# Weight blocks converted step by step inside the attention, its results in a ring outside the pool

## The chip, the core and the metric

The kernel runs on one core of a Trainium2 chip. The core has five engines that each take their instructions in program order and meet only through semaphores: TensorE (PE in the profile, its weight loads PEld), VectorE (DVE), ScalarE (ACT), GpSimd (POOL) and SyncE (SP), which here issues nearly all DMAs. The metric is the time of one execution on the device in microseconds. A run varies by some tenths of a per cent; about 1% is taken as what separates a change from none.

## What is computed

Three stages follow one another: attention with capped scores, a gated MLP, and a mixture of experts.

```python
def _attn_ref(q, k, v, cap):                  # 4 batches, 12 heads, 448 tokens, 64 wide
    scores = cap * np.tanh(scale * q @ k.T / cap)
    attn = np.exp(scores - max); attn /= attn.sum(-1) + 1e-9
    return attn @ v

def _moe_ref(x, w_in, w_out):                 # 1792 tokens, 768 -> 2048 -> 768
    h = x @ w_in
    return (h * (1.0 / (1.0 + np.exp(-h)))) @ w_out

def _moe2_ref(x, w_skip, w_gate, w1, w2):     # 8 experts, one for each token
    ...
```

The MLP's weights arrive as 64-bit floats. The kernel reads them as pairs of 32-bit words and makes 32-bit floats of them on the chip.

## The kernel before

**Attention.** Two heads form a `Unit` (24 units: 4 batches of 6). Two units form a quad of 7 chunks; a `Chunk4` is 128 keys of both heads of a unit, or the 64 keys that are left over from both units. `slot4(p)` handles two chunks, and there are `SL` = 42 slots with scores. In a slot ScalarE does `weigh` (tanh, then exp, of 128 x 896 values, for each of two chunks); TensorE does `av` of the slot before, the denominators (`den`) of units whose sums are made, and the scores of the next slot; VectorE does a first sum (`sum1`), reciprocals of denominators and the products `xf` (`finish`), and, for the first two batches, a cast `x_h`; GpSimd does the second sum (`sum2`), the sums of the leftover keys (`sum_rest`) and, for the first two batches, the subtraction `x_l`. So a unit's denominator on TensorE needs sums from VectorE and GpSimd of the slot before. For batches 2 and 3 `xf` is stored to `xd` in DRAM by SyncE. The instructions are issued in the order in which the code is written; nothing reorders them. The engines keep that order.

**Precision.** A matmul of the MLP is made of three, with a high and a low part of weights and data: `wh` times `x_h`, `wh` times `x_l`, `wl` times `x_h`.

**Conversion of a weight block.** `fetch` loads the 64-bit block `raw` (768 KB, 2 buffers). `ready` makes `wr` (3 buffers): magnitude on ScalarE (line 392), clamp on VectorE (393), scaling of the low word on ScalarE (394), shift and mask on VectorE (396), sign on VectorE (397), and an add on GpSimd (398). `split` stores `wr` for later use (`keep`), casts it to `wh` on ScalarE (407) and subtracts on GpSimd to `wl` (410). `tick_a(k)` splits block k+1, `tick_b(k)` makes block k+3 ready and fetches block k+5. Each call issues the whole conversion at once. In the attention this happens for blocks 0 to 2 at slots 31, 34 and 38, with fetches at 28 and 29.

**From the attention to the MLP.** After the last slot with scores come the first MLP matmuls, `h_start(0,0,0)` (18 matmuls of block 0 with batch 0), then `slot4(SL)`, the last chunks' products and sums, `h_start(0,0,1)` and `slot4(SL + 1)`, the last denominator. `h_end` makes of such a result `ph` the pair `gh`, `gl`: tanh on ScalarE, a product on VectorE, a cast on ScalarE, a subtraction on VectorE. Then the attention's pool `ap`, where `xf` lies in two buffers, is closed, and pools for `gh` and `gl` are opened in the space that came free. `h_end(0,1)` is the first to write there. A ring is a piece of a tile in the pool `mp`, which lives on, taken in turn by `turn_of`; the ring `xt` has four places of 448 columns, and before the change only the MLP's second half uses it.

The rest of the program, MLP and experts, is not touched.

Of the kernel before, what the change touches and what calls it, by code (L numbers as in the profile page):

```python
# [1 line left out]

# [6 lines left out]
F32 = mybir.dt.float32  # L9
F32R = mybir.dt.float32r  # L10
I32 = mybir.dt.int32
U32 = mybir.dt.uint32
AF = mybir.ActivationFunctionType
ALU = mybir.AluOpType
AX = mybir.AxisListType

P = 128
B, H, S, D = 4, 12, 448, 64
# [20 lines left out]
WC = DM  # L39
# [20 lines left out]
def kernel(  # L60
# [13 lines left out]
    nc = tc.nc  # L74
# [17 lines left out]
    def turn_of(t):  # L92
        ring = scr[t]
        ring[3] = (ring[3] + 1) % ring[2]
        return ring[0][:, ring[3] * ring[1] : (ring[3] + 1) * ring[1]]
# [28 lines left out]
    class Unit:  # L124
# [72 lines left out]
            nc.vector.reciprocal(self.rd, pden[:, :S])  # L197

        def finish(self):
            xf = ap.tile([P, S], F32, tag="xf", name=f"xf{self.n}")  # L200
            nc.vector.tensor_tensor(xf, self.pav[:, :S], self.rd, op=ALU.mult)
            self.xf = xf
            if self.b >= 2:
                nc.sync.dma_start(xd[self.b - 2, self.hp], xf)
# [139 lines left out]
    def slot4(p):  # L344
        for c in chunks4[2 * p : 2 * p + 2]:
            c.weigh()
        late = chunks4[2 * p - 2 : 2 * p] if p else []
        for c in late:
            c.av()
        due = open_[:]  # L350
        open_.clear()
        for c in late:
            if (u := c.sums()) is not None:
                open_.append(u)
        closing()
        for u in due:
            u.den()
            done.append(u)
        for c in chunks4[2 * p + 2 : 2 * p + 4]:
            c.score()  # L360
        for c in chunks4[2 * p : 2 * p + 2]:
            quad = c.i // (2 * KF + 1)
            for u in units[2 * quad + 2 : 2 * quad + 4]:
                if c.c == 0:
                    u.load()
                elif c.c == KF:
                    u.load_v()

    class Chunk:
# [30 lines left out]
        def split(self):  # L400
            if self.wh is not None:
                return
            w = self.width
            if self.first:
                nc.sync.dma_start(self.keep, self.wr[:, :w])
            self.wh = wp.tile([P, WC], F32R, tag="wh", name=f"wh{self.n}")
            nc.scalar.copy(self.wh[:, :w], self.wr[:, :w])  # L407
            self.wl = wp.tile([P, WC], F32R, tag="wl", name=f"wl{self.n}")
            eng = nc.gpsimd if self.first else nc.vector
            eng.tensor_tensor(self.wl[:, :w], self.wr[:, :w], self.wh[:, :w], op=ALU.subtract)  # L410

    K1, K2 = NF + ND * NQ, 2 * (NF + ND * NQ)
    wq = {}
# [10 lines left out]
    def at(k):  # L424
        return chunks[k] if 0 <= k < len(chunks) else None

    def tick_a(k):
        if at(k + 1):
            at(k + 1).split()

    def tick_b(k):
        if k < K1 - 1:
            at(k + 3).ready()
            if k < K1 - 3:
                at(k + 5).fetch()
        elif k < K1:
            pass
        elif k == K1:
            gp3s.close()
            conv.close()  # L440
            gp2s.close()
            wq["p"] = front.enter_context(tc.tile_pool(name="wq", bufs=4))
            for i in range(2, 6):
                at(K1 + i).ready()
        elif at(k + 5):
            at(k + 5).ready()
# [6 lines left out]
    def h_start(k, f, b, ph):  # L453
        c_ = at(k)
        n = 0
        for c in range(ND):
            for w_, x_ in ((c_.wh, xh), (c_.wh, xl), (c_.wl, xh)):
                nc.tensor.matmul(  # L458
                    ph, w_[:, c * P : (c + 1) * P], x_[b, c], start=(n == 0), stop=(n == 3 * ND - 1)
                )  # L460
                n += 1
# [5 lines left out]
    def h_end(f, b, ph):  # L467
        e = turn_of("e")
        nc.scalar.activation(e, ph, AF.Tanh, scale=0.5)
        nc.vector.scalar_tensor_tensor(e, e, 1.0, ph, op0=ALU.add, op1=ALU.mult)  # L470
        pool = gp0 if f < 2 and b != 1 else gpool["last" if b == 1 and f == NF - 1 else b]
        h = pool.tile([P, S], F32R, tag=f"gh{f}", name=f"gh{b}_{f}")
        nc.scalar.copy(h, e)  # L473
        l = pool.tile([P, S], F32R, tag=f"gl{f}", name=f"gl{b}_{f}")
        nc.vector.tensor_tensor(l, e, h, op=ALU.subtract)  # L475
        gt[f, b] = h, l
# [718 lines left out]
    chunks4[0].score()  # L1195
    chunks4[1].score()
    SL = N4 // 2
    for p in range(SL):
        slot4(p)
        if SL - 14 <= p < SL - 12:  # L1200
            at(p - (SL - 14)).fetch()
        elif p == SL - 11:
            tick_b(-3)
        elif p == SL - 8:
            tick_a(-1)
            tick_b(-2)
        elif p == SL - 4:
            tick_b(-1)
    ph = ps_s.tile([P, 2, 512], F32, tag="psc", name="ph_0")
    h_start(0, 0, 0, ph[:, 0, :S])  # L1210
    slot4(SL)
    tick_a(0)
    ph1 = h_bank(0, 1)
    h_start(0, 0, 1, ph1)
    h_end(0, 0, ph[:, 0, :S])
    slot4(SL + 1)
    tick_b(0)
    closing()
# [383 lines left out]
```

## Time and profile before

| | us |
|---|---|
| median of 3 runs | 828.13 (827.52 to 832.83) |
| the profiled execution | 827.55 |
| its span, first to last instruction | 825.8 |
| PE busy | 772.4 (94%) |
| DVE busy | 448.8 (54%) |
| ACT busy | 425.0 (51%) |
| POOL busy | 309.0 (37%) |

An engine's busy time is the time its instructions ran, a wait counts as idle, but an instruction that is held up after its start counts as busy. Matmuls are pipelined, so the times given for single ones overlap. The stages by time: attention to about 186 us, a stretch with both attention and MLP to 212.5 us, the MLP to about 695 us, then the experts. TensorE's granted clock is given as a share of its full rate.

### The profile page before, as it was taken

How to read it: one execution, taken by the hardware profiler on the slowest of the kernel's cores; microseconds unless marked ns; L12 is line 12 of the kernel's file. 1: busy time of each engine (PE TensorE's matmuls, PEld its weight loads, DVE VectorE, ACT ScalarE, POOL GpSimd, SP SyncE). 2: the span in 40 equal slices, each digit the busy share in tenths (PEclk: the TensorE clock that was granted, in tenths of full speed). 3: DMA queues.
4: the chain of work that ended last, by engine and by line, in shares of the span. 5: the costliest groups of instructions: out<-in, count | busy, mean ns of one | idle time of the engine just before them, and what ended most of it. 6: DMA issues, size and time to landing. Idle time of an engine off the chain costs nothing.

```text
span 825.8 us, 11325 instructions
## 1 busy us (share of the span) xinstructions
PE 772.4 (94%) x4066; PEld 583.4 (71%) x4066; DVE 448.8 (54%) x659; ACT 425.0 (51%) x591; POOL 309.0 (37%) x217
## 2 busy tenths in 40 slices
PE   7999998688799999999999999999999999689786
PEld 2333332236699999988988999888999887478563
DVE  2788877665677765444334674333664333482431
ACT  7999999692566654444433543333454221341510
POOL 3798876753555544444540220000200000430530
PEclk9999999999799999999999999999999999799989
DMA  6333336412576655675755427965364652686360
GB/s 195 102 101 100 92 128 200 146 62 61 149 217 190 194 150 144 202 210 177 216 178 166 124 86 245 281 212 162 119 221 165 199 147 89 208 319 262 96 220 21
DMA packets 78099, 135.34 MB, mean 164 GB/s; under 512 B 8630, under 2 KB 47926, under 8 KB 78018
## 3 DMA queue, kind: packets, MB, share of 16 engines
q1 hardware_dynamic: 76514, 130.34, 50.7%
q0 software_dynamic: 1504, 4.00, 1.4%
q8 instruction: 41, 0.67, 0.4%
q14 instruction: 40, 0.33, 0.1%
HBM read 108.17 MB, written 31.01 MB: 169 GB/s over the span
## 4 chain that ended last, share of the span: by engine, by line
PE 62%; DMA 6%; issue 3%; DVE 2%; POOL 1%; ACT 0%; SPq 0%; POOLq 0%; DVEq 0%; ACTq 0%
PE py L483 28%; PE ph L458 27%; DMA xg<-xs,ids 4%; PE py L963 2%; PE ph L920 2%; PE pt L495 1%; PE pl L517 1%; DMA table<-slotd,si 1%; DMA scr_e<-xd 1%; DMA scr_xo<-xs,idg 1%; DVE base L731 0%; DMA out_dram<-scr_xt,ids 0%; POOL xg L812 0%; PE pr L592 0%; PE px L884 0%
## 5 line engine op out<-in xcount | busy, mean ns | idle before, releaser
L458 PE MATMUL ph<-x,whi 128*128 128x448 f32 x768 | 219.8, 368 | 7.4 <-ACT whi L407 6.7
L458 PEld LDWEIGHTS ph<-x,whi 128*128 128x128 f32 x768 | 144.8, 190 | 21.3 <-ACT whi L407 7.0
L483 PE MATMUL py<-gh,who 128*128 128x448 f32 x384 | 143.5, 374 | 0.1
L458 PE MATMUL ph<-x,wli 128*128 128x448 f32 x384 | 140.5, 366 | 0.8 <-POOL wli L410 0.8
L483 PE MATMUL py<-gh,wlo 128*128 128x448 f32 x384 | 141.1, 367 | 0.1
L483 PE MATMUL py<-gl,who 128*128 128x448 f32 x384 | 140.8, 367 | 0.0
L637 POOL DMA_INDIRECT table<-slotd,si x16 | 17.7, 1109 | 236.7 <-DVE si L627 138.7
L197 DVE RECIPROCAL rd<-pden 128x448 f32<-128x448 f32 x24 | 70.9, 2955 | 36.9 <-PE pden L195 36.6
L239 ACT ACTIVATE a<-a,capt 128x896 f32<-128x896 f32 x84 | 87.6, 1042 | 2.7
L238 ACT ACTIVATE a<-psc,tsc 128x896 f32<-128x896 f32 x84 | 83.0, 989 | 8.6 <-PE psc L142 8.4
L473 ACT CAST gh<-scr_e 128x448 fp32r<-128x448 f32 x64 | 36.4, 568 | 87.6 <-DVE scr_e L470 75.6
L407 ACT CAST who<-wro 128x512 fp32r<-128x512 f32 x72 | 44.6, 621 | 71.6 <-PE py L483 64.6
L483 PEld LDWEIGHTS py<-gh,who 128*128 128x128 f32 x384 | 72.1, 188 | 11.1 <-ACT who L407 2.6
L475 DVE TENSOR_TENSOR gl<-scr_e,gh 128x448 fp32r<-128x448 f32 x64 | 52.4, 820 | 47.5 <-ACT gh L473 47.5
L483 PEld LDWEIGHTS py<-gh,wlo 128*128 128x128 f32 x384 | 72.1, 188 | 7.6 <-DVE wlo L410 0.9
L458 PEld LDWEIGHTS ph<-x,wli 128*128 128x128 f32 x384 | 72.8, 190 | 6.5 <-POOL wli L410 1.4
L142 PE MATMUL psc<-q,k 64*128 64x448 f32 x288 | 70.1, 595 | 7.1 <-DMA q<-in_q_dram 4.1
L483 PEld LDWEIGHTS py<-gl,who 128*128 128x128 f32 x384 | 72.2, 188 | 6.2
L171 PE MATMUL pav<-a,vt 128*64 128x448 f32 x288 | 63.4, 554 | 0.0
L410 DVE TENSOR_TENSOR wlo<-wro,who 128x512 fp32r<-128x512 f32 x48 | 33.0, 689 | 54.7 <-ACT who L407 52.9
L142 PEld LDWEIGHTS psc<-q,k 64*128 64x128 f32 x288 | 24.9, 193 | 51.4 <-ACT a L238 18.7
L158 POOL TENSOR_TENSOR sm<-sm,a 64x448 f32<-64x448 f32 x48 | 55.2, 1151 | 15.5 <-DVE sm L146 12.3
(256 smaller groups left out, 1115.4 us busy)
## 6 DMA issues: line engine op xcount, KB each, us to landing
raw64i<-in_moe_w_in_dram SPq DMA_DIRECT2D x16, 768.0 KB, 5.3
raw64o<-in_moe_w_out_dram SPq DMA_DIRECT2D x24, 512.0 KB, 4.2
wri<-ws_in SPq DMA_DIRECT2D x32, 384.0 KB, 3.7
wro<-ws_out SPq DMA_DIRECT2D x48, 256.0 KB, 3.1
xs<-scr_xo SPq DMA_DIRECT2D x36, 224.0 KB, 4.6
s<-in_moe_w_dram SPq DMA_DIRECT2D x7, 1024.0 KB, 4.9
ws_in<-wri SPq DMA_DIRECT2D x16, 384.0 KB, 5.7
ws_out<-wro SPq DMA_DIRECT2D x24, 256.0 KB, 4.7
```

Source lines behind the costliest of these rows:

```text
L142: nc.tensor.matmul(psc[:, j, :S], self.k[r, c * P : (c + 1) * P], self.q[r, :], start=True, stop=True)
L158: nc.gpsimd.tensor_tensor(self.sm[r, q_], self.sm[r, q_], rest[r, o : o + S], op=ALU.add)
L171: nc.tensor.matmul(self.pav[r, :S], self.vt[:, c * 2 + j, :], self.a[c][:, q_], start=(c == 0 and self.hp % 2 == 0), stop=(c == KF - 1 and ...
L197: nc.vector.reciprocal(self.rd, pden[:, :S])
L238: nc.scalar.activation(a.rearrange("p (j s) -> p j s", j=2), self.psc[:, :, :S], AF.Tanh, scale=tsc)
L239: nc.scalar.activation(a, a, AF.Exp, scale=capt)
L407: nc.scalar.copy(self.wh[:, :w], self.wr[:, :w])
L410: eng.tensor_tensor(self.wl[:, :w], self.wr[:, :w], self.wh[:, :w], op=ALU.subtract)
L458: nc.tensor.matmul(ph, w_[:, c * P : (c + 1) * P], x_[b, c], start=(n == 0), stop=(n == 3 * ND - 1))
L473: nc.scalar.copy(h, e)
L475: nc.vector.tensor_tensor(l, e, h, op=ALU.subtract)
L483: nc.tensor.matmul(py[:, :S], w_[:, c * P : (c + 1) * P], g_, start=(hf + c + st == 0), stop=(hf == NQ - 1 and c == QC - 1 and st == 2),)
```

## The change

The conversion of blocks 0 to 2 gets two generators, `steps` and `split_steps`. They do the same arithmetic as `ready` and `split`, but ScalarE has no part in it: the magnitude is max(-x, x) on VectorE, the clamp is on GpSimd, the scaling of the low word and the cast to `wh` are on VectorE. Each step is one instruction, or two where a GpSimd add follows. From slot 2 on, every second slot is followed by one step: `n` counts these, n = 0 at slot 2, n = 10 at slot 22, and so on. Block 0 is converted in steps 0 to 4 (slots 2 to 10), block 1 in 5 to 9 (slots 12 to 20), block 0 is split in 10 and 11 (22, 24), block 2 converted in 12 to 16 (26 to 34), block 1 split in 17 and 18 (36, 38). Fetches stand at slots 2, 12, 22 and 36. Block 2 is split as before, by `tick_a(1)`.

`xf` is now a place in the ring `xt`. And `h_end(0, 0)` stands ahead of `slot4(SL)`; `tick_a(0)`, which split block 1, is gone.

```diff
         def finish(self):
-            xf = ap.tile([P, S], F32, tag="xf", name=f"xf{self.n}")
+            xf = turn_of("xt")
...
+        def steps(self):
+            w = self.width
+            self.wr = cp.tile([P, WC], F32, tag="wr", bufs=3, name=f"wr{self.n}")
+            hi, lo = self.raw[:, :w, 1], self.raw[:, :w, 0]
+            wi, mag = self.wr.bitcast(I32)[:, :w], self.wr[:, :w]
+            top = hi.bitcast(F32)
+            nc.vector.scalar_tensor_tensor(mag, top, -1.0, top, op0=ALU.mult, op1=ALU.max)
+            yield
+            nc.gpsimd.tensor_scalar(mag, mag, F64_LEAST, F64_MOST, op0=ALU.max, op1=ALU.min)
+            yield
+            nc.vector.tensor_scalar(lo, lo.bitcast(U32), 2.0**-29, None, op0=ALU.mult)
+            yield
+            nc.vector.tensor_scalar(wi, wi, 3, 0x3FFFFFFF, op0=ALU.logical_shift_left, op1=ALU.bitwise_and)
+            yield
+            nc.vector.scalar_tensor_tensor(wi, hi, -(1 << 30), wi, op0=ALU.bitwise_and, op1=ALU.bitwise_or)
+            nc.gpsimd.tensor_tensor(wi, wi, lo, op=ALU.add)
+            yield
+
+        def split_steps(self):
+            w = self.width
+            nc.sync.dma_start(self.keep, self.wr[:, :w])
+            self.wh = wp.tile([P, WC], F32R, tag="wh", name=f"wh{self.n}")
+            nc.vector.tensor_copy(self.wh[:, :w], self.wr[:, :w])
+            yield
+            self.wl = wp.tile([P, WC], F32R, tag="wl", name=f"wl{self.n}")
+            nc.gpsimd.tensor_tensor(self.wl[:, :w], self.wr[:, :w], self.wh[:, :w], op=ALU.subtract)
+            yield
...
+    early = itertools.chain(at(0).steps(), at(1).steps(), at(0).split_steps(), at(2).steps(), at(1).split_steps())
+    begun = {0: (0, 1), 5: (2,), 10: (3,), 17: (4,)}
     for p in range(SL):
         slot4(p)
-        if SL - 14 <= p < SL - 12:
-            at(p - (SL - 14)).fetch()
-        elif p == SL - 11:
-            tick_b(-3)
-        elif p == SL - 8:
-            tick_a(-1)
-            tick_b(-2)
-        elif p == SL - 4:
-            tick_b(-1)
+        n, odd = divmod(p - 2, 2)
+        if n >= 0 and not odd:
+            for i in begun.get(n, ()):
+                at(i).fetch()
+            next(early, None)
...
     h_start(0, 0, 0, ph[:, 0, :S])
+    h_end(0, 0, ph[:, 0, :S])
     slot4(SL)
-    tick_a(0)
     ph1 = h_bank(0, 1)
     h_start(0, 0, 1, ph1)
-    h_end(0, 0, ph[:, 0, :S])
     slot4(SL + 1)
```

The order of instructions on GpSimd around slots 10 to 14, before the change (`sm` is a unit's sums, `a` a chunk's exponentials, `x` the low part of the attention's result):

```order
L158 TENSOR_TENSOR sm_5_474<-sm_5_474,a_409 64x448 x2
L149 TENSOR_TENSOR sm_5_474<-sm_5_474,a_464 128x896
L214 TENSOR_TENSOR x_306<-xf_4_509,x_306 128x448
L149 TENSOR_TENSOR sm_0_531<-sm_0_531,a_500 128x896
L158 TENSOR_TENSOR sm_0_531<-sm_0_531,a_521 64x448 x2
L214 TENSOR_TENSOR x_306<-xf_5_564,x_306 128x448
L158 TENSOR_TENSOR sm_1_584<-sm_1_584,a_521 64x448 x2
L149 TENSOR_TENSOR sm_1_584<-sm_1_584,a_552 128x896
L214 TENSOR_TENSOR x_625<-xf_0_623,x_625 128x448
```

The same place after it (`wri_0` and `wri_1` are blocks 0 and 1 in 32 bits, `raw64i_0` the loaded words):

```order
L159 TENSOR_TENSOR sm_5_479<-sm_5_479,a_415 64x448 x2
L428 TENSOR_TENSOR wri_0_263<-wri_0_263,raw64i_0_259 128x768
L150 TENSOR_TENSOR sm_5_479<-sm_5_479,a_469 128x896
L215 TENSOR_TENSOR x_311<-scr_xt,x_311 128x448
L150 TENSOR_TENSOR sm_0_537<-sm_0_537,a_507 128x896
L159 TENSOR_TENSOR sm_0_537<-sm_0_537,a_527 64x448 x2
L215 TENSOR_TENSOR x_311<-scr_xt,x_311 128x448
L159 TENSOR_TENSOR sm_1_593<-sm_1_593,a_527 64x448 x2
L150 TENSOR_TENSOR sm_1_593<-sm_1_593,a_562 128x896
L421 TENSOR_SCALAR wri_1_557<-wri_1_557 128x768
L215 TENSOR_TENSOR x_634<-scr_xt,x_634 128x448
```

The add that completes block 0 now stands between the two sums of one unit, and the clamp of block 1 ahead of a subtraction.

VectorE around slots 8 to 12, before (`rd` is the reciprocal of the denominators `pden`, `pav` the product with the values):

```order
L197 RECIPROCAL rd_3_426<-pden_3_423 128x448
L201 TENSOR_TENSOR xf_3_454<-pav_3_351,rd_3_426 128x448
L209 CAST x_306<-xf_3_454 128x448
L146 SCALAR_TENSOR_TENSOR sm_5_474<-a_438,eps,a_441 128x896
L197 RECIPROCAL rd_4_481<-pden_4_478 128x448
L201 TENSOR_TENSOR xf_4_509<-pav_4_412,rd_4_481 128x448
L209 CAST x_306<-xf_4_509 128x448
L146 SCALAR_TENSOR_TENSOR sm_0_531<-a_467,eps,a_497 128x896
L197 RECIPROCAL rd_5_537<-pden_5_534 128x448
```

And after:

```order
L198 RECIPROCAL rd_3_431<-pden_3_428 128x448
L425 TENSOR_SCALAR wri_0_263<-wri_0_263 128x768
L202 TENSOR_TENSOR scr_xt<-pav_3_357,rd_3_431 128x448
L210 CAST x_311<-scr_xt 128x448
L147 SCALAR_TENSOR_TENSOR sm_5_479<-a_444,eps,a_447 128x896
L198 RECIPROCAL rd_4_486<-pden_4_483 128x448
L427 SCALAR_TENSOR_TENSOR wri_0_263<-raw64i_0_259,wri_0_263 128x768
L202 TENSOR_TENSOR scr_xt<-pav_4_418,rd_4_486 128x448
L210 CAST x_311<-scr_xt 128x448
L147 SCALAR_TENSOR_TENSOR sm_0_537<-a_472,eps,a_504 128x896
L198 RECIPROCAL rd_5_543<-pden_5_540 128x448
L419 SCALAR_TENSOR_TENSOR wri_1_557<-raw64i_1_261 128x768
```

A step stands behind a reciprocal and ahead of the product `xf` of the slot after.

VectorE where the attention ends, before (`scr_e` and `gl` belong to `h_end`, `sm_5` is the last unit's first sum):

```order
L201 TENSOR_TENSOR xf_3_1396<-pav_3_1283,rd_3_1373 128x448
L146 SCALAR_TENSOR_TENSOR sm_5_1422<-a_1360,eps,a_1381 128x896
L197 RECIPROCAL rd_4_1430<-pden_4_1427 128x448
L470 SCALAR_TENSOR_TENSOR scr_e<-scr_e,ph_1399 128x448
L475 TENSOR_TENSOR gl_0_1460<-scr_e,gh_0_1458 128x448
L201 TENSOR_TENSOR xf_4_1462<-pav_4_1342,rd_4_1430 128x448
L197 RECIPROCAL rd_5_1468<-pden_5_1465 128x448
```

And after:

```order
L202 TENSOR_TENSOR scr_xt<-pav_3_1276,rd_3_1357 128x448
L499 SCALAR_TENSOR_TENSOR scr_e<-scr_e,ph_1382 128x448
L504 TENSOR_TENSOR gl_0_1405<-scr_e,gh_0_1403 128x448
L147 SCALAR_TENSOR_TENSOR sm_5_1411<-a_1344,eps,a_1365 128x896
L198 RECIPROCAL rd_4_1419<-pden_4_1416 128x448
L202 TENSOR_TENSOR scr_xt<-pav_4_1327,rd_4_1419 128x448
L198 RECIPROCAL rd_5_1445<-pden_5_1442 128x448
```

`h_end`'s two instructions now stand ahead of the last unit's first sum instead of behind it and a reciprocal.

## Rows read from the trace of the kernel before

**Rows 1.** Chain that ended last, in time order: start, length in us, what.

```profile
212.50 103.25 PE ph L458 x502
```

**Rows 2.** Timeline of ScalarE: start and length in us, line, output<-input, count.

```profile
6.21 0.99 ACT L238 ACTIVATE a<-psc,tsc 128x896 f32<-128x896 f32 x1
...
94.81 0.99 ACT L238 ACTIVATE a<-psc,tsc 128x896 f32<-128x896 f32 x1
...
132.44 0.90 ACT L392 ACTIVATE wri<-raw64i 128x768 f32<-128x768 f32 x1
...
184.21 0.99 ACT L238 ACTIVATE a<-psc,tsc 128x896 f32<-128x896 f32 x1
```

**Rows 3.** ScalarE's waits to 200 us: total us, times, longest.

```profile
ACT a L238 <- PE psc L142: 8.4, 3, 6.2
```

**Rows 4.** Timeline, a denominator on TensorE; brackets: idle before it, releaser.

```profile
159.96 1.76 PE L195 MATMUL pden<-sm,ones 128*64 128x448 f32 x4 [4.80 <-POOL sm L149]
```

**Rows 5.** Busy time by stretch: length, PE, PEld, DVE, ACT, POOL, clock, DMA.

```profile
6.20:37.70 31.50, 31.04 (x156) 9.19 (x152) 14.60 (x20) 30.98 (x33) 19.84 (x14) 1.00 0.49 150
...
65.30:92.90 27.60, 27.58 (x152) 8.71 (x144) 23.94 (x17) 27.14 (x30) 24.07 (x17) 1.00 0.34 101
...
160.00:170.00 10.00, 10.00 (x44) 3.21 (x44) 4.73 (x3) 6.34 (x7) 5.17 (x4) 0.83 0.36 132
```

**Rows 6.** Timeline in the first half: sums, a denominator, subtractions.

```profile
65.04 2.10 POOL L149 TENSOR_TENSOR sm<-sm,a 128x896 f32<-128x896 f32 x1
...
67.20 0.97 PE L195 MATMUL pden<-sm,ones 128*64 128x448 f32 x4
...
69.13 1.13 POOL L214 TENSOR_TENSOR x<-xf,x 128x448 fp32r<-128x448 f32 x1 [1.99 <-PE psc L142]
...
72.40 2.38 POOL L158 TENSOR_TENSOR sm<-sm,a 64x448 f32<-64x448 f32 x2
...
73.71 2.02 DVE L146 SCALAR_TENSOR_TENSOR sm<-a,eps,a 128x896 f32<-128x896 f32 x1
...
74.86 1.87 POOL L214 TENSOR_TENSOR x<-xf,x 128x448 fp32r<-128x448 f32 x1
```

**Rows 7.** Timeline, instructions of a conversion and a memset on GpSimd.

```profile
134.57 0.56 DVE L396 TENSOR_SCALAR wri<-wri 128x768 int32<-128x768 int32 x1
...
135.16 0.96 DVE L397 SCALAR_TENSOR_TENSOR wri<-raw64i,wri 128x768 int32<-128x768 int32 x1
...
136.35 1.84 POOL L398 TENSOR_TENSOR wri<-wri,raw64i 128x768 int32<-128x768 int32 x1 [4.01 <-DVE wri L397]
...
212.38 0.53 POOL L1061 MEMSET scr_xo<- 112x512 f32 x1
```

**Rows 8.** Timeline in the second half: a sum and the denominator that needs it.

```profile
118.66 2.09 POOL L149 TENSOR_TENSOR sm<-sm,a 128x896 f32<-128x896 f32 x1
...
122.54 0.92 PE L195 MATMUL pden<-sm,ones 128*64 128x448 f32 x4
```

**Rows 9.** Timeline from the attention's end to the MLP (SPq: DMA issue by SyncE).

```profile
184.80 1.14 DVE L146 SCALAR_TENSOR_TENSOR sm<-a,eps,a 128x896 f32<-128x896 f32 x1
...
188.52 2.08 POOL L149 TENSOR_TENSOR sm<-sm,a 128x896 f32<-128x896 f32 x1
...
188.67 0.54 ACT L469 ACTIVATE scr_e<-ph 128x448 f32<-128x448 f32 x1 [1.67 <-PE ph L458]
...
194.78 0.97 PE L195 MATMUL pden<-sm,ones 128*64 128x448 f32 x4
...
201.66 0.61 DVE L470 SCALAR_TENSOR_TENSOR scr_e<-scr_e,ph 128x448 f32<-128x448 f32 x1
...
203.66 0.38 SPq L204 DMA_DIRECT2D xd<-xf  x1
...
209.24 0.56 ACT L473 CAST gh<-scr_e 128x448 fp32r<-128x448 f32 x1 [12.06 <-DMA xd<-xf]
...
212.50 0.74 PE L458 MATMUL ph<-x,wli 128*128 128x448 f32 x1 [0.80 <-POOL wli L410]
...
218.37 0.57 PE L458 MATMUL ph<-x,whi 128*128 128x448 f32 x2
```

More of the change, by code (lines that the diff above doesn't have):

```diff
@@ L1 @@
+import itertools
 from contextlib import ExitStack
@@ L1197 @@
     SL = N4 // 2
+    early = itertools.chain(at(0).steps(), at(1).steps(), at(0).split_steps(), at(2).steps(), at(1).split_steps())
+    begun = {0: (0, 1), 5: (2,), 10: (3,), 17: (4,)}
     for p in range(SL):
         slot4(p)
-        if SL - 14 <= p < SL - 12:
-            at(p - (SL - 14)).fetch()
-        elif p == SL - 11:
-            tick_b(-3)
-        elif p == SL - 8:
-            tick_a(-1)
-            tick_b(-2)
-        elif p == SL - 4:
-            tick_b(-1)
+        n, odd = divmod(p - 2, 2)
[3 more added lines that the diff above has]
+            next(early, None)
+    assert next(early, 0) == 0
     ph = ps_s.tile([P, 2, 512], F32, tag="psc", name="ph_0")
     h_start(0, 0, 0, ph[:, 0, :S])
+    h_end(0, 0, ph[:, 0, :S])
     slot4(SL)
-    tick_a(0)
     ph1 = h_bank(0, 1)
     h_start(0, 0, 1, ph1)
-    h_end(0, 0, ph[:, 0, :S])
     slot4(SL + 1)
```

## Prediction

> **What bounds the kernel now.** I read the chain that ended last first. From 212.50 us on it is TensorE alone for hundreds of matmuls [rows 1]: whatever delays or advances that start moves the end by as much. So the question is when the MLP's matmuls can run unhindered, and I went backwards from there. The timeline of ScalarE shows what fills the time before. The first tanh of the attention starts at 6.21 us, the 46th at 94.81 us and the 84th (the last) at 184.21 us [rows 2]. The first 45 steps take 88.60 us, 1.969 us each, back to back: ScalarE sets the pace. At that pace the 84th tanh would start at 6.21 + 83 x 1.969 = 169.6 us; it starts **14.6 us** later. Of these, 8.4 us are ScalarE waiting for scores from TensorE [rows 3]; the remaining 6.2 us are nearly all the seven instructions that the conversion puts on ScalarE (six such as the 0.90 us at 132.44 us in rows 2, and one cast). The scores were late because TensorE, in order, waited for a denominator's sums, the longest time 4.80 us for GpSimd [rows 4]; GpSimd was late because its conversion add and the sums behind it stand in one queue.
>
> What is left of slack on VectorE and GpSimd is read in a table by stretch. Over 27.60 us in the first half GpSimd is busy 24.07 and VectorE 23.94 us [rows 5]. That looks like 87%, but the two get in each other's way. A sum on VectorE issued at 73.71 us takes 2.02 us; GpSimd's pair of sums before it ends at 72.40 + 2.38 = 74.78 us, and the VectorE sum ends 0.95 us after that. GpSimd's subtraction, issued at 74.86 us, then takes 1.87 us, while the same one at 69.13 us, with nothing beside it, takes 1.13 [rows 6]. They take turns: a VectorE sum costs GpSimd 0.74 us, to VectorE 0.95. A period is 7 slots (14 chunks, 27.56 us) and holds 4 units. GpSimd's own work in it is 4 x (2.10 + 2.38 + 1.13) = 22.4 us; four VectorE sums take 3.0 to 3.8, four casts 0 to 1.3 (the one-input conversion step's 0.56 us [rows 7] x 448/768, or nothing where a cast slips into a gap). Together **25.4 to 27.5 of 27.56 us**: 0 to 2.2 us of room. That it is near 0 shows at 67.14 us, where GpSimd ends a sum (65.04 + 2.10) and the denominator that needs it starts at 67.20 us [rows 6].
>
> The Trainium skill's page "SBUF — State Buffer", section "Who interferes with whom", says that whichever of the two engines starts first holds the shared port pair for its whole instruction, two-input VectorE instructions included. The trace's 1.87 against 1.13 us shows the blocking, though for less than a whole instruction; by the page's whole instructions the room would be at the low end, 0, and the first-half price below 2.2 us higher.
>
> **The change, part by part.**
>
> *Off ScalarE and out of the late attention: the 14.6 us go.* Abs, scale and two casts leave ScalarE, and the three bunched conversions leave slots 31 to 41 (counting slots of 3.94 us from 6.21 us). This is only a gain as far as the new places cost less.
>
> *First half, slots 2 to 24: the new price.* Up to slot 7 I price at nothing: in 6.20 to 37.70 us GpSimd is busy 19.84 and VectorE 14.60 of 31.50 us [rows 5], which covers an abs, a clamp and a scale (under 4 us); and VectorE's wait for the first raw block is covered by its idle time there. If that cover fails it is at most those 4 us. From slot 8 to slot 22 the steps fall into the two full periods: `wi` 0.56, combine 0.96, GpSimd add 1.84 [rows 7], abs 0.96 (taken as the combine, also two inputs), clamp 1.3, scale 0.5, then again 0.56 + 0.96 + 1.84, and a cast 0.67 (between the 0.56 and the 0.96): 10.2 us. The clamp on GpSimd is not in the trace: it is bounded by the memset, 0.53 us x 768/512 = 0.80 us, and the two-input add, 1.84; I take the middle. The scale has a strided input: 0 (if it does not block GpSimd) to 0.96. Room takes off 0 to 2.2 us per period, I take 1.1, since the denominator at 67.20 us had none: 10.2 - 2.2 = **8.0 us** lost by ScalarE, bounds 5 (room 4.4, cheap clamp and scale) and 11. It arises so: a late GpSimd sum holds the denominator, TensorE's scores stand behind it, ScalarE waits for scores. The first place is slot 10: the new add stands in GpSimd's queue ahead of a unit's sum and must itself wait for VectorE's combine, which stands behind a reciprocal on VectorE.
>
> *Second half, slots 24 to 41.* No cast or subtraction per unit any more, so a period needs 4 x (2.10 + 2.38) + 3.8 = 21.7 of 27.56 us. The third block's steps and both `wl` subtractions (together about 10.5 us at the prices above) fit into over two periods with 5.8 us of room each. Locally the worst is slot 34, combine and add together 2.8 us ahead of a sum; the comparable sum ended at 118.66 + 2.09 = 120.75 us and was needed at 122.54 [rows 8], 1.8 us of slack. So **1.0 us**, bounds 0 and 3.
>
> Attention: 14.6 - 8.0 - 1.0 = **5.6 us** gained.
>
> *The end of the attention: a DMA wait that goes.* In ScalarE's order `gh` of the second batch waited 12.06 us, to 209.24 us, for the store of the last `xf`, issued at 203.66 us [rows 9]: the tile lies where the attention's pool was. Behind it in the queue stand the casts of the third weight block, and TensorE waited for these, starting unhindered only at 212.50 us; and the 16 matmuls left of that group's 18 ran until 218.37 us, 0.37 us each, where the chain has 103.25 / 502 = 0.21 [rows 1, 9]. With `xf` in the ring the cast waits only for loads that are long done, the last denominator and its own input. In exchange `h_end(0,0)` is now ahead of slot 42: on VectorE, the last unit's first sum, at 184.80 us today, stands behind the tanh at 188.67 us (0.54) and three instructions up to `gl`, each about the 0.61 us of the one at 201.66. It starts at about 188.67 + 0.54 + 0.1 + 1.8 = 191.1, 6.3 us later. GpSimd's sums of that unit end 188.52 + 2.08 = 190.60 us today, so 196.9 then; TensorE needs them at 194.78 [rows 9]. **2.1 us** of idle TensorE, a new wait. Everything after, its two groups of matmuls and VectorE's reciprocal, shifts by that: VectorE's `e`, done at 202.27 us today, at about 204.4, then `gh` 0.56 [rows 9], the cast of the weight block about 0.8 (as many elements as the 0.90 us of rows 2, or as VectorE's 0.56), GpSimd's subtraction 1.8 (as its add in rows 7): it could run unhindered from about 207.1 instead of 212.50 us. That is 5.4 us, and with the clock at its higher level 16 x 0.16 = 2.6 us more: **8.0 us** gained, bounds 4.5 (if the clock still falls, and 1 us more wait) and 10 (no new wait).
>
> Sum: 827.55 (the profiled execution; span 825.8) - 5.6 - 8.0 = 813.9 us. The median of the runs is 828.13, 0.6 higher, so **814.5 us**.
>
> **Rivals.**
>
> 1. *The steps hide* (an engine busy 87% has room, turns or not). Then only the second half's 1 us and about 1 us more remain: 14.6 - 2 + 8.0 = 20.6, **807.5 us**. For it: single steps, and sums that can be early outside the tight denominators. Against: 67.14 to 67.20 us.
> 2. *The new layout doesn't remove the wait*: `gh` or the weight cast behind it meets another late one, such as VectorE's queue, in which the last unit's sum, two reciprocals and the third block's successor now stand close. Then the 8.0 us are lost: **822.5 us**, inside 1%. Against: the weight block itself is done slots earlier.
> 3. *Slower: TensorE's clock falls in the first half.* After the 4.80 us wait the four matmuls of a denominator took 1.76 us where they take 0.97 at 67.20 us, and the granted clock is 0.83 from 160 to 170 us, so for part of it the lower of the two levels, 1.2 instead of 2.4 GHz [rows 4 to 6]. TensorE is full in the attention; at the lower level a slot would take about half as long again, 2.0 us more. From 7 slots at that level the gain is gone, from 11 it is over 1% slower; were it all 17 slots from 8 to 24, **848 us**. For it: every late denominator now interrupts TensorE. Against: steps are at most 2.8 us long, so no single wait like that one.
>
> **How the numbers follow.** Forecast 0.55, rival 1 0.22, rival 2 0.14, rival 3 0.09. The forecast's own bounds, 5 to 11 and 0 to 3 and 4.5 to 10, make 808 to 822 if not all fall together. The range reaches to rivals 1 and 2: 806 to 823 us; left out are rival 3 and what lies outside the bounds, together under 0.2. About 1%, 8.3 us, is what a measurement of this kernel can tell from no change: faster means under 819.8. The forecast (0.50 of its 0.55) and rival 1 lie there: 0.72. Within 1%: the forecast's rest, rival 2 and a mild rival 3, 0.22. Slower: 0.06.
>
> **What would show it.** Right: no ScalarE wait for the `xf` store and a gap in TensorE of about 2 us before the last denominator; denominators from slot 10 to 24 waiting for GpSimd, ScalarE waits of about 8 us before 105 us, the 84th tanh near 178.6 us. Wrong: no ScalarE wait in the first half (rival 1); a late `gh` (rival 2); granted clock under 1.00 before 105 us (rival 3). A clamp or abs far outside its bounds would make the prediction wrong too.

## The result, and the profile after

| | before | after |
|---|---|---|
| median, us | 827.83 (825.66 to 832.83, 4 runs) | 816.17 (814.34 to 819.36, 4 runs) |
| ratio | | 0.9843 (95% interval 0.9809 to 0.9877) |
| the profiled execution | 827.55, span 825.8 | 814.34, span 812.6 |

The forecast was 814.5 us, between 806 and 823, so the measured 816.17 us lies inside. The direction and the mechanism at the attention's end came as reckoned; the price of the first half did not: it was put at 8.0 us and came to 11.8.

The chain of the kernel after, as in [rows 1] (start, length, what). TensorE runs unhindered 7.1 us earlier, and the same 502 matmuls take 100.68 instead of 103.25 us, 2.6 us less:

```profile
205.41 100.68 PE ph L487 x502
```

The 2.6 us are the clock. Busy time by stretch as in [rows 5], the same stretch before, then after; the figure to read is the third from the end, the granted clock, 0.97 and 1.00:

```profile
212.50:315.70 103.20, 103.20 (x503) 96.58 (x504) 76.10 (x103) 61.35 (x101) 53.71 (x30) 0.97 0.62 177
```

```profile
212.50:315.70 103.20, 103.20 (x517) 96.73 (x517) 76.76 (x105) 61.79 (x102) 56.10 (x31) 1.00 0.64 184
```

ScalarE after, as in [rows 2] (line numbers are one higher): the first, 46th, 55th and last tanh, with the waits for scores between them. The number in brackets is the idle time ahead.

```profile
6.36 0.99 ACT L239 ACTIVATE a<-psc,tsc 128x896 f32<-128x896 f32 x1
...
43.17 1.01 ACT L239 ACTIVATE a<-psc,tsc 128x896 f32<-128x896 f32 x1 [1.28 <-PE psc L143]
...
60.34 1.01 ACT L239 ACTIVATE a<-psc,tsc 128x896 f32<-128x896 f32 x1 [1.31 <-PE psc L143]
...
73.93 1.01 ACT L239 ACTIVATE a<-psc,tsc 128x896 f32<-128x896 f32 x1 [1.67 <-PE psc L143]
...
83.31 1.01 ACT L239 ACTIVATE a<-psc,tsc 128x896 f32<-128x896 f32 x1 [1.39 <-PE psc L143]
...
101.05 0.99 ACT L239 ACTIVATE a<-psc,tsc 128x896 f32<-128x896 f32 x1
...
108.40 1.01 ACT L239 ACTIVATE a<-psc,tsc 128x896 f32<-128x896 f32 x1 [5.29 <-PE psc L143]
...
124.45 0.99 ACT L239 ACTIVATE a<-psc,tsc 128x896 f32<-128x896 f32 x1
...
182.20 0.99 ACT L239 ACTIVATE a<-psc,tsc 128x896 f32<-128x896 f32 x1
```

I use one yardstick below: the **lag** of the 55th tanh, which lies just behind the first half. At ScalarE's pace of 1.969 us it starts 54 x 1.969 = 106.3 us after the first. Here it starts at 124.45, so the lag is 124.45 - 6.36 - 106.3 = 11.8 us; 8.0 was forecast for the first half. From there to the 84th it takes 57.75 us where the pace gives 29 x 1.969 = 57.1: 0.65 lost, against 1.0. The waits summed, as in [rows 3] (total, times, longest), for TensorE and for ScalarE: TensorE waits for GpSimd's sums, and ScalarE for TensorE's scores.

```profile
PE pden L196 <- POOL sm L150: 10.8, 6, 4.1
...
ACT a L239 <- PE psc L143: 11.5, 6, 5.3
```

The longest of these, in the timeline of GpSimd, VectorE and TensorE after. The add that completes block 1 (L428) stands ahead of the leftover sums and the second sum of one unit; everything up to the denominator then comes late:

```profile
97.21 2.69 POOL L428 TENSOR_TENSOR wri<-wri,raw64i 128x768 int32<-128x768 int32 x1
...
99.99 3.09 POOL L159 TENSOR_TENSOR sm<-sm,a 64x448 f32<-64x448 f32 x2
...
103.15 2.10 POOL L150 TENSOR_TENSOR sm<-sm,a 128x896 f32<-128x896 f32 x1
...
105.31 1.25 PE L196 MATMUL pden<-sm,ones 128*64 128x448 f32 x4 [4.15 <-POOL sm L150]
```

Behind this wait the granted clock fell. The stretch in the kernel after, and in its second profile (e11):

```profile
103.00:112.00 9.00, 6.69 (x28) 2.23 (x30) 4.95 (x5) 3.65 (x5) 8.37 (x7) 0.81 0.39 147
```

```profile
103.00:112.00 9.00, 6.50 (x24) 1.89 (x24) 5.17 (x5) 3.15 (x4) 7.75 (x6) 0.62 0.40 150
```

The clamps on GpSimd after; three instructions, of which the second is lengthened by a VectorE sum that ran until 72.85 us:

```profile
26.81 2.80 POOL L421 TENSOR_SCALAR wri<-wri 128x768 f32<-128x768 f32 x1
...
71.88 3.60 POOL L421 TENSOR_SCALAR wri<-wri 128x768 f32<-128x768 f32 x1
...
133.19 2.77 POOL L421 TENSOR_SCALAR wri<-wri 128x768 f32<-128x768 f32 x1
```

The attention's end after, as in [rows 9]: the last unit's first sum, the last denominator with its new wait, and the cast `gh` of the second batch, which no longer waits for a store but for its input on VectorE.

```profile
188.53 1.15 DVE L147 SCALAR_TENSOR_TENSOR sm<-a,eps,a 128x896 f32<-128x896 f32 x1
...
194.37 1.55 PE L196 MATMUL pden<-sm,ones 128*64 128x448 f32 x4 [1.95 <-POOL sm L150]
...
202.14 0.57 ACT L502 CAST gh<-scr_e 128x448 fp32r<-128x448 f32 x1 [9.13 <-DVE scr_e L499]
```

### The profile page after: what moved, and what is told of

Its sections match the earlier page's. It is cut to its first block, busy times and chain, and to the rows that moved or that the text cites. A ratio compares the mean times of both kernels' runs of the same rounds, so it can differ in the third digit from the quotient of the medians.

```text
span 812.6 us, 11311 instructions
## 1 busy us (share of the span) xinstructions
PE 770.3 (95%) x4066; PEld 580.5 (71%) x4066; DVE 459.1 (56%) x664; ACT 418.4 (51%) x583; POOL 321.9 (40%) x220
## 4 chain that ended last, share of the span: by engine, by line
PE 69%; DMA 7%; POOL 7%; issue 6%; ACT 5%; DVE 4%; SPq 0%; POOLq 0%; DVEq 0%
PE py L512 29%; PE ph L487 27%; DMA xg<-xs,ids 4%; ACT a L239 3%; PE psc L143 2%; POOL sm L150 2%; POOL sm L159 2%; PE py L992 2%; PE pav L172 2%; DVE rd L198 2%; ACT a L240 2%; DMA xraw<-in_moe_w_dram 2%; PE pden L196 1%; PE pt L524 1%; PE ph L949 1%
## 5 line engine op out<-in xcount | busy, mean ns | idle before, releaser
L504 DVE TENSOR_TENSOR gl<-scr_e,gh 128x448 fp32r<-128x448 f32 x64 | 54.7, 855 | 40.7 <-ACT gh L502 39.4
L159 POOL TENSOR_TENSOR sm<-sm,a 64x448 f32<-64x448 f32 x48 | 57.5, 1199 | 21.3 <-DVE sm L147 18.4
```

What stands on the lines that cost most here:

```text
L159: nc.gpsimd.tensor_tensor(self.sm[r, q_], self.sm[r, q_], rest[r, o : o + S], op=ALU.add)
```

## The experiments

All figures but the medians and ratios are from each run's one profile. "To MLP" is the time from the 84th tanh to the start of the 502 matmuls. The ratio is to the kernel before, run beside it on the same chip (medians 829.15 to 829.72 us there): e1 to e4 on one chip, e5 to e8 and e12 on a second, e9 to e11 on a third.

| run | median, us | ratio (95%) | lag, us | 84th tanh | to MLP | 502 matmuls |
|---|---|---|---|---|---|---|
| before | 827.83 | 1 | 0.2 | 184.21 | 28.29 | 103.25 |
| e12 before again | 828.64 | 0.9993 (0.9973 to 1.0014) | 0.9 | 186.83 | 29.72 | 103.03 |
| after | 816.17 | 0.9843 (0.9809 to 0.9877) | 11.8 | 182.20 | 23.21 | 100.68 |
| e11 changed again | 816.44 | 0.9845 (0.9815 to 0.9875) | 12.5 | 183.10 | 23.09 | 100.70 |
| e1 clamp on VectorE | 814.21 | 0.9811 (0.9772 to 0.985) | 9.6 | 180.11 | 23.41 | 100.68 |
| e2 ring alone | 819.63 | 0.9893 (0.9851 to 0.9934) | 0.3 | 184.38 | 21.39 | 100.68 |
| e3 steps alone | 828.17 | 0.9985 (0.996 to 1.001) | 12.0 | 182.40 | 29.55 | 103.38 |
| e4 late, VectorE clamp | 810.85 | 0.9777 (0.9739 to 0.9814) | 0.2 | 177.38 | 22.87 | 100.67 |
| e5 add one slot later | 814.56 | 0.9833 (0.9787 to 0.9879) | 9.2 | 180.42 | 22.61 | 100.68 |
| e6 clamp of one operation | 814.23 (1 run) | | 11.4 | 181.64 | 23.08 | 100.67 |
| e7 h_end in old place | 815.26 | 0.9828 (0.9793 to 0.9864) | 13.1 | 183.55 | 21.07 | 100.69 |
| e8 places chosen | 808.75 | 0.977 (0.972 to 0.982) | 0.5 | 174.95 | 21.06 | 100.69 |
| e9 no GpSimd add | 810.93 | 0.9779 (0.9744 to 0.9814) | 5.6 | 175.59 | 23.20 | 100.67 |
| e10 places by sum | 805.13 | 0.9697 (0.9661 to 0.9732) | 0.8 | 174.04 | 20.96 | 104.01 |

**e1, the clamp.**

```diff
-            nc.gpsimd.tensor_scalar(mag, mag, F64_LEAST, F64_MOST, op0=ALU.max, op1=ALU.min)
+            nc.vector.tensor_scalar(mag, mag, F64_LEAST, F64_MOST, op0=ALU.max, op1=ALU.min)
```

> The changed kernel, the clamp alone moved from GpSimd to VectorE. Theory A (the price of the first half is the GpSimd clamp: it took 2.80, 3.60 and 2.77 us where 1.3 was reckoned): the two clamps of the first half become about 0.5 us each on VectorE, ScalarE waits some 4 us less before 110 us, the 84th tanh starts near 178 us instead of 182.2, time about 812 us. Theory B (the place counts, any step ahead of a sum holds it up; the longest wait, 5.29 us at 108.40, stands behind an add): the waits stay near 11 us, 84th tanh 181 to 183, time 815 to 817.

VectorE takes 0.50 to 0.55 us for the clamp:

```profile
68.57 0.50 DVE L421 TENSOR_SCALAR wri<-wri 128x768 f32<-128x768 f32 x1
```

The lag fell by 2.2 us (2.9 against the changed kernel's second profile), not by 4. The waits at 43.17 and 83.31 us are gone, those at 60, 73 and 108 us are there still, the last at 5.80 us. So theory A was half right: the clamp is a cost, but four fifths of the lag is something else. The medians' intervals overlap; it is the rows that tell the two apart.

**e2 and e3, the two halves of the change.** e2 is the kernel before with this alone:

```diff
-            xf = ap.tile([P, S], F32, tag="xf", name=f"xf{self.n}")
+            xf = turn_of("xt")
```

> The kernel before with xf in the ring and nothing else. Theory A (the wait for the store of xf is what held the MLP back, the forecast's 'no new wait' case of 10 us): the 12.06 us wait of gh is gone, the chain's unhindered part starts near 203 to 205 us instead of 212.5, time 818 to 820 us. Theory B (gh meets another late one, or the gain needs h_end ahead of the last slot): unhindered from 209 us or later, time 823 to 828.

e3 is the changed kernel with that line undone.

> The changed kernel with xf back in the attention's pool: the steps and the moved h_end remain. Theory A (the ring brings the gain at the end, the steps only 2 us): 84th tanh near 182.2, gh waits again for the store of the last xf, about 2 us less than before at most, since the last denominator is 2 us later: 826 to 828 us. Theory B (moving h_end or the split of the second block off the end brings it): unhindered from 206 to 208 us, time 816 to 820.

The chains, e2 first, then e3:

```profile
205.77 100.68 PE ph L458 x502
```

```profile
211.95 103.38 PE ph L487 x502
```

And e3's `gh` of the second batch on ScalarE, which waits again for a transfer, now 15.5 us (the row names the store of a weight block, issued at 203.52 us; that of `xf` stands directly before it, at 203.09):

```profile
208.69 0.56 ACT L502 CAST gh<-scr_e 128x448 fp32r<-128x448 f32 x1 [15.50 <-DMA ws_in<-wri]
```

The mechanism of theory A holds in both, with two figures just past what was expected: e2 started at 205.77 us (203 to 205), e3's median is 828.17 us (826 to 828). In e2 the same cast starts at 202.51 us and waits for no transfer, before either store is issued (203.74 and 204.18 us), so the wait comes from the place of `xf` and not from the weight block's store. The ring alone brings 1.07% of the time, about 9 us. The steps alone bring nothing that can be measured, though their attention ends 1.8 us earlier than in the first profile of before: 1.3 us of that are given back at the end, where the last denominator waits 2.04 us, as it does in the kernel after. On top of the ring the steps bring about 0.5% (0.9893 to 0.9843), and the two intervals overlap.

**e4, the steps in the second half.** On top of e1:

```diff
-    begun = {0: (0, 1), 5: (2,), 10: (3,), 17: (4,)}
+    begun = {-3: (0, 1), 5: (2,), 10: (3,), 17: (4,)}
...
-        n, odd = divmod(p - 2, 2)
-        if n >= 0 and not odd:
-            for i in begun.get(n, ()):
-                at(i).fetch()
+        n = p - (SL - 19)
+        for i in begun.get(n, ()):
+            at(i).fetch()
+        if n >= 0:
             next(early, None)
```

> The kernel of the first run (clamp on VectorE) with the 19 steps in slots 23 to 41, one in each slot, none in the first half. Theory A (GpSimd and VectorE have no room while the casts and subtractions of the first two batches run, and some after): no ScalarE wait before 95 us, 46th tanh near 94.9 us; the steps in the second half take about 20 us of the two engines where 2.7 periods with 5.8 us of room each have 16, so some 4.5 us are lost: 84th tanh 172 to 176 us, time 806 to 811. Theory B (any step ahead of a sum holds a denominator up, wherever it stands): a step in every slot costs as much as in every second, 84th tanh 178 us or later, time 812 or more.

The 55th tanh is at 112.91 us, a lag of 0.2: with no step in the first half nothing is lost there. In the second half 7.4 us are lost, 5.89 of them in one wait, where again an add stands ahead of one unit's leftover sums and second sum (118.48 us, 2.64 us):

```profile
127.11 1.76 PE L196 MATMUL pden<-sm,ones 128*64 128x448 f32 x4 [4.25 <-POOL sm L150]
...
130.72 1.01 ACT L239 ACTIVATE a<-psc,tsc 128x896 f32<-128x896 f32 x1 [5.89 <-PE psc L143]
```

So the first half came as theory A has it; the 84th tanh, at 177.38 us, lies between A (172 to 176) and B (178), and the median, 810.85 us, in A's range. Steps cost in the second half too, but mainly at one place. That is where theory C comes from.

**e5, the place of the adds.** In the changed kernel the add is kept back and issued behind the next, odd slot.

```diff
-            nc.gpsimd.tensor_tensor(wi, wi, lo, op=ALU.add)
+            sums_due.append((wi, lo))
...
             next(early, None)
+        elif sums_due:
+            wi, lo = sums_due.pop()
+            nc.gpsimd.tensor_tensor(wi, wi, lo, op=ALU.add)
```

> The changed kernel; only the three GpSimd adds that complete a block stand one slot later (slots 11, 21, 35 instead of 10, 20, 34). Theory C (formed after the first runs: what costs is an add right ahead of the slot of the period in which one unit's leftover sum and second sum follow each other and the next denominator is due; the 4 to 5 us wait of TensorE stood behind that one place in four kernels): the waits of 1.50 us at 58.37 and of 4.15 us at 105.31 go or shrink below 1 us each, 84th tanh 177 to 179 us, time 811 to 813. Theory A (GpSimd and VectorE have no room in the first half, wherever the work stands): the waits move to other denominators, the sum stays at 9 us or more, 84th tanh 181 to 183, time 815 to 817.

Neither came out. Denominators of e5: the 4.15 us became 1.13, and another wait, 1.47 us before, became 2.75.

```profile
72.94 1.76 PE L196 MATMUL pden<-sm,ones 128*64 128x448 f32 x4 [2.75 <-POOL sm L150]
...
103.21 0.97 PE L196 MATMUL pden<-sm,ones 128*64 128x448 f32 x4 [1.13 <-POOL sm L150]
```

The lag is 2.6 us less, 9.2. The worst place is worth that; the rest moves to other denominators, as theory A says. The wait of 2.75 us also shows the clock at work: the granted clock was 0.66 from 72 to 77 us, and ScalarE's wait behind it is 4.63 us.

**e6, the price of the clamp by itself.** `F64_MOST, op0=ALU.max, op1=ALU.min` becomes `None, op0=ALU.max`.

> The changed kernel with a clamp of one operation instead of two (only the lower bound; the upper one is left out). What a GpSimd clamp of 128x768 costs, by itself: if the second operation costs, 1.3 to 1.9 us instead of 2.8; if the form costs (an operand of one tensor with constants), 2.5 to 2.8 as before.

```profile
26.60 2.15 POOL L421 TENSOR_SCALAR wri<-wri 128x768 f32<-128x768 f32 x1
...
132.62 2.13 POOL L421 TENSOR_SCALAR wri<-wri 128x768 f32<-128x768 f32 x1
```

Between the two expectations: the second operation costs 2.77 - 2.13 = 0.64 us, and with one operation the clamp is still longer than the two-input add of 1.84 [rows 7], which the prediction had taken for the upper bound. (The third clamp, not shown, took 2.96 us beside a VectorE instruction; its like took 3.60 in the kernel after.)

**e7, `h_end(0, 0)`.** The line goes back behind `h_start(0, 0, 1, ph1)`.

> The changed kernel with h_end(0,0) back in its old place, behind the second group of matmuls. If the 1.95 us wait of TensorE ahead of the last denominator is the price of the moved h_end and lies on the path (the forecast's 2.1 us): the wait goes, the unhindered part of the chain starts near 203.5 instead of 205.4 us, time 814 to 815. If it is covered, because gh needs the earlier h_end more: start 205 or later, time 816 to 818.

The wait ahead of the last denominator is gone, and the way from the 84th tanh to the MLP is 21.07 instead of 23.21 us: the moved `h_end` costs 2.1 us. The start itself, 204.62 us, is only 0.8 earlier, because this execution's 84th tanh came 1.35 us later; the granted clock from 103 to 112 us was 0.62 in it and 0.81 in the other. The median, 815.26 us, lies in neither range expected and cannot be told from the 816.17 us of the kernel after; the rows carry this reading.

**e9, no conversion step on GpSimd in the first half.** On top of e1; the scale step falls away and the add becomes

```diff
-            nc.gpsimd.tensor_tensor(wi, wi, lo, op=ALU.add)
+            nc.vector.scalar_tensor_tensor(wi, lo, 29, wi, op0=ALU.logical_shift_right, op1=ALU.bitwise_or)
```

> The first run's kernel (clamp on VectorE, steps at the places of the change) with scale and GpSimd add replaced by one VectorE instruction that shifts the low word and puts it in with an or (the last bit is cut off instead of rounded). GpSimd has no conversion step left in the first half. Theory A (the two engines take turns, so a step costs its duration on either): per block 1.84 + 0.55 us go and 0.95 come, two blocks: some 3 us less than the 9.6 us lost by the 55th tanh, which then starts near 119.5 us, the 84th near 177.5, time 811 to 812. Theory C (GpSimd adds ahead of sums made the waits; VectorE's steps hide): the waits of 1.51 and 4.43 us go, 55th tanh 113 to 116 us, 84th 171 to 174, time 806 to 808.

The 55th tanh started at 118.34 us, the 84th at 175.59: nearer to A (119.5 and 177.5) than to C. The lag is 5.6 us, nearly all of it in two waits of ScalarE, 2.65 us at 72.18 and 2.42 us at 102.30, and GpSimd's first step, a subtraction, comes only at 112.44 us: VectorE's steps alone hold GpSimd's sums up. The second of the two waits shows one way in which they do it. Two steps, 1.89 us (at 90.85) and 1.78 us long where the same two later take 0.95 and 0.98 (at 148.16 and 149.14), stand in VectorE's queue ahead of a first sum, and GpSimd is idle for 2.05 us until it has that sum:

```profile
92.78 1.78 DVE L427 SCALAR_TENSOR_TENSOR wri<-raw64i,wri 128x768 int32<-128x768 int32 x1
...
94.48 1.14 DVE L147 SCALAR_TENSOR_TENSOR sm<-a,eps,a 128x896 f32<-128x896 f32 x1
...
95.79 2.32 POOL L159 TENSOR_TENSOR sm<-sm,a 64x448 f32<-64x448 f32 x2 [2.05 <-DVE sm L147]
...
100.32 0.97 PE L196 MATMUL pden<-sm,ones 128*64 128x448 f32 x4 [2.40 <-POOL sm L150]
```

Ahead of the first wait GpSimd has no such gap from 58.30 to 70.15 us; there its own instructions are lengthened (a pair of leftover sums 2.99 us instead of 2.33).

**e8 and e10, places chosen.** The steps stand in slots 22 to 41 by a table; `h_end` is in its old place. e8 keeps the add on GpSimd, as a step of its own, and the clamp is on VectorE; the fetches move with the steps (slots 19, 29, 33 and 40):

```diff
...
+    plan = {22: "0", 23: "0", 24: "0", 25: "0", 26: "0", 27: "1", 28: "0 1", 29: "1", 30: "1", 31: "1", 32: "1",
+            33: "2 s0", 34: "2", 35: "s0", 36: "2", 37: "2", 38: "2", 39: "2", 40: "s1", 41: "s1"}
...
```

> All three findings together: clamp on VectorE, h_end in the old place, and the steps only from slot 22 on, with the adds and subtractions of GpSimd at slots 28, 32, 35, 39 and 41 where its queue had gaps of 1.5 to 2.6 us, and the add two slots behind its input where it can be. Theory C: no wait of TensorE for GpSimd over 1 us, 84th tanh 170 to 173 us, unhindered from 192 to 195 us, time 802 to 806. Theory A (the second half has 16 us of room for 20 us of steps): 84th tanh 174 to 177, time 807 to 811.

Theory A came out: two waits for GpSimd, of 1.48 and 2.39 us, where C allowed none over 1 us, the 84th tanh at 174.95 us and a median of 808.75 us, both in A's ranges; the start, 196.01 us, is past C's 192 to 195. Two stretches of e8 (length, busy PE, PEld, DVE, ACT, POOL, then clock and DMA):

```profile
112.00:132.00 20.00, 18.52 (x99) 5.86 (x98) 20.00 (x14) 18.21 (x19) 15.00 (x10) 1.00 0.42 131
132.00:160.00 28.00, 25.61 (x136) 8.21 (x134) 28.00 (x18) 25.16 (x26) 21.23 (x14) 1.00 0.63 199
```

VectorE is busy without a gap, 48 of 48 us; the rows show that much of it is being held up. A scaling step starts 0.21 us after a sum on GpSimd that ends at 108.67 + 2.10 = 110.77 us, and ends 0.42 us after that. The same step takes 0.55 us where nothing holds it up (e1, at 32.63 us), and the shift and mask behind it, with GpSimd idle, 0.54:

```profile
108.67 2.10 POOL L150 TENSOR_TENSOR sm<-sm,a 128x896 f32<-128x896 f32 x1
108.88 2.31 DVE L423 TENSOR_SCALAR raw64i<-raw64i 128x768 int32<-128x768 uint32 x1
...
111.64 0.54 DVE L425 TENSOR_SCALAR wri<-wri 128x768 int32<-128x768 int32 x1
```

e10 takes the one VectorE instruction of e9 and puts VectorE's steps in pairs where the next slot has no first sum (the last subtraction stands behind slot 42, the fetches at slots 19, 27, 32 and 39):

```diff
...
+    plan = {22: "0 0", 24: "0 0", 26: "0 1", 29: "1 1", 31: "1 1", 33: "s0 2", 35: "s0", 36: "2 2", 38: "2 2", 40: "s1"}
...
```

> The kernel of chosen places without any GpSimd add (the one VectorE instruction instead), and VectorE's steps in pairs only where no first sum is next in its queue; GpSimd subtracts at slot 35 and behind slot 42. In the kernel of chosen places VectorE was busy without a gap from 112 to 160 us, steps of 0.5 us lasting up to 2.3 beside GpSimd's sums, and two denominators waited 1.5 and 2.4 us. Theory A (turns): 15 steps and 2 casts of 0.5 to 0.95 us plus their waits fit into 16 us of room: no wait of TensorE over 1 us, 84th tanh 170 to 173, time 803 to 806. Rival (a VectorE step waits for a whole GpSimd sum and carries the delay to the next sum, wherever it stands): waits stay at 3 to 5 us, time 807 to 810.

One wait of 1.99 us is left, where theory A allowed none over 1 us, and the 84th tanh missed A's 173 by 1 us; the median of 805.13 us is in A's range and the lowest of all, 3.0% below before (0.9661 to 0.9732). The profiled execution is this kernel's longest (810.37 us): its 502 matmuls took 104.01 us, evenly slower (147 in the 30 us from 240 us on, where e8 has 152) at a granted clock of 1.00. Why is not known.

**e11 and e12, the spread.**

> The changed kernel unaltered, to see how much its own profile and time differ from one execution to the next: the 84th tanh was at 182.20 us and the time 816.2; both are expected within 1.5 us of that, and the part behind the first 502 matmuls, 506.5 us, may come out up to 4 us longer, as in the other kernels (507.5 to 510.1).

> The kernel before unaltered, to see how much its own profile differs between executions: the chain of the profiles gives the change 9 to 10 us, the medians 13. If the profiled execution of before was one of its faster ones, another shows a part that varies (the granted clock behind TensorE's wait of 6.7 us, or the part behind the first 502 matmuls, 510.05 us) longer by 2 to 4 us; if not, the chain comes out within 1 us of it everywhere.

The part behind the first 502 matmuls is 510.05 us in the first profile of before, 829.3 - 216.55 - 103.03 = 509.7 in the second, 506.5 and 816.7 - 206.19 - 100.70 = 509.8 in the two of after. So 3.5 us of the 13.2 between the first two profiles were this execution's own, in a part that the change does not touch: that its 814.34 us lies so near the forecast of 814.5 is luck. Before differs from itself too: the 84th tanh was 2.6 us later in e12. Of these, 1.1 us were there at the 55th tanh already; the other 1.5 came behind the long wait for a denominator, which was the same (4.81 us), but the granted clock behind it was not; before first, then e12:

```profile
160.00:187.00 27.00, 24.07 (x115) 8.91 (x116) 17.29 (x12) 21.92 (x23) 16.40 (x11) 0.94 0.31 106
```

```profile
160.00:187.00 27.00, 22.94 (x96) 7.07 (x100) 16.01 (x11) 19.43 (x21) 16.64 (x11) 0.82 0.28 98
```

## Why the prediction was right, and where it was not

**What bounds the kernel: right.** In every run the chain is TensorE's from the start of the 502 matmuls on, and what lies behind them took 506.5 to 510.1 us, wherever they started.

**Off ScalarE, 14.6 us: right.** ScalarE has no conversion step in the attention any more. From the 55th to the 84th tanh, where the bunched conversions stood, 14.4 us were lost before and 0.65 are lost after.

**First half, 8.0 us with bounds 5 and 11: too small, and just outside.** Measured 11.8, and 12.5 in e11. Four parts of this step failed.
- *The clamp, 1.3 us.* It was bounded by the add, 1.84 us, and took 2.77 to 2.80. Its move to VectorE gave 2.2 to 2.9 us back (e1). This is the mis-sized term. A clamp far outside its bounds had been named as a sign of being wrong, and this one was outside; the time still came out inside the range, because the miss is some 4 us and the range 17 us wide.
- *The scale, 0.5 us, at most 0.96.* Beside a GpSimd sum it took 1.50 us (at 78.81 us), with nothing beside it 0.55 (e1): it is held up like the others.
- *Slots 2 to 7 at nothing.* The busy times of [rows 5] did cover the steps, but not their turns: the clamp at 26.81 us pushed GpSimd's sums back, and the first denominator to wait was that at 41.20 us, two slots earlier than said (ScalarE's 1.28 us at 43.17). In e1 this wait is gone.
- *The clock behind a long wait.* The add ahead of two sums of one unit gave TensorE 4.15 us of waiting; the granted clock was 0.81 from 103 to 112 us in after and 0.62 in e11, and ScalarE's wait grew to 5.29 and 5.82: 1.1 to 1.6 us more than TensorE's, where at 43, 60 and 74 us the two differ by 0.2 us at most. That is rival 3 in small, one slot or two instead of seventeen. The ground against rival 3, that steps of at most 2.8 us make no single wait like that of 4.80, did not hold: the add and the sums behind it add up.

These parts overlap: 1.3 us of what e1 gives back had been priced, and the wait of slots 2 to 7 is in it. So 0.9 to 1.6 us, at least, for the clamp and 1.1 to 1.6 for the clock were missing, 2.0 to 3.2 of the 3.8 to 4.5 us; the rest is not split. What the step said of the mechanism stands: there is no room in the first half. e9 shows it best, where VectorE's steps alone cost 5.6 us (VectorE's queue is as much a part of it as GpSimd's); e5 shows that moving an add mostly moves the wait. The claim that VectorE and GpSimd take turns is now shown from the other side, by e8's step of 2.31 us. The Trainium skill, page "SBUF — State Buffer", section "Who interferes with whom", says that whichever of the two engines issues first keeps the shared port pair for its whole instruction. Those rows agree, and with the whole instructions of that rule the prediction's own price, 8.0 + 2.2 = 10.2 us, would have been nearer to 11.8; the 0.74 us that the prediction read in [rows 6] fits the rest of a VectorE sum that had its turn already (it ran until 73.71 + 2.02 = 75.73 us, the subtraction was issued at 74.86).

**Second half, 1.0 us: right** (0.65). That holds for the few steps that stand there and for their places: with all 19 in it, one in every slot, the second half lost 7.4 us (e4), with all at chosen places 4.2 and 3.5 (e8, e10).

**Attention, 5.6 us: too large.** It was 2.0 between the first two profiles and 186.83 - 183.10 = 3.7 between the second two.

**The attention's end, 8.0 us: right, in each part.** No wait for a store; a new wait of 1.95 us (2.1 forecast) ahead of the last denominator; the clock's 2.6 us; and the way to the MLP, 207.1 - 184.21 = 22.9 us by the forecast, was 23.21 and 23.09. (The terms written out there, 204.4 + 0.56 + 0.8 + 1.8, make 207.6 and not 207.1, so a way of 23.4 us and a gain of 7.5; the measured way lies between the two.) The gain is 5.1 + 2.6 = 7.7 us by the first two profiles, 6.6 + 2.3 = 8.9 by the others. e2 against e3 shows that it is the ring's. What the prediction did not say is that the change pays 2.1 us of this for the moved `h_end` and gets nothing for it (e7).

**The sum.** With the measured terms of the first profiles it would have been 827.55 - 2.0 - 7.7 = 817.9 us, with those of the second pair, from e12's profiled execution, 830.98 - 3.7 - 8.9 = 818.4, which is e11's (818.41). The medians, 816.17 and 816.44, lie between these and the forecast.

**The rivals.** Rival 1 (the steps hide) falls with the lag of 11.8 us, rival 2 with the `gh` row; rival 3 came in the small form above, its sign (a granted clock under 1.00) behind the wait that ended at 105.31 us, where 105 us had been named. Of ScalarE's waits, put at about 8 us before 105 us, 5.7 us came before it and 5.3 in the one that ended at 108.40.

Left open: how e9's 5.6 us split over the single VectorE steps, what else the first half's missing 4 us hold, and why the clock behind one and the same wait falls for longer in one execution than in another.

## What to carry to other kernels

Two engines that take turns have less room than their idle time shows: price a step there by its duration plus the wait for the other engine's instruction, and look at which late consumer stands at the end of either engine's queue, since moving a step mostly moves the wait. Where a tile in a scratch pool is still being stored when the pool's space is reused, a place in a longer-lived ring removes the wait for the store, and that was worth more here (1.07%) than all steps as the change placed them (about 0.5% on top). Where the steps stand, and on which engine, counted for more still: with places chosen in the second half and no add on GpSimd, the same ring and the conversion together bring 3.0% (e10, which also has `h_end` in its old place and cuts a last bit off instead of rounding). Do not bound an operation by one of another form; where it is unknown, the far bound belongs further out.

## What the runs showed of the hardware that was not expected

- GpSimd's clamp of 128x768 took 2.77 to 2.80 us with two operations and 2.13 to 2.15 with one, its two-input add of the same size 1.84, VectorE's clamp 0.50 to 0.55, each with nothing beside it.
- A VectorE step of about half a microsecond takes up to 2.31 us beside a GpSimd sum, and counts as busy all that time.
- Behind a wait of TensorE of 4.15 to 4.81 us the granted clock fell in every profile here that has one. How much differs from one execution to the next (0.94 and 0.82 from 160 to 187 us in two executions of before; the stretch from that wait to the attention's end was 1.5 us longer in the second). Behind shorter waits it fell in some and not in others: 0.91 from 112 to 132 us around the 1.99 us of e10, but 1.00 from 155 to 165 us around the 2.39 us of e8.
